# Feed-forward blocks of a Conformer layer: VectorE's work placed block by block, step d one block later, two buffers for normalised keys, chunk 1 transposed on TensorE

## The chip, the cores and the metric

The kernel runs on one core of a Trainium2 chip. Time is device microseconds of one launch, from its start to the last store. The core has five engines that each run their own instructions strictly in program order: TensorE (PE, matmuls), VectorE (DVE), ScalarE (ACT, activations), GpSimd (POOL) and SyncE (SP, which here issues nearly all DMAs). They meet through semaphores; in this kernel a small layer of code (class `Sync`) derives each wait from the buffers that an operation reads and writes.

## The reference

One Conformer layer over B = 2 sequences of T = 4000 tokens, D = 512 features, F = 2048 hidden, bf16 inputs. `ln` is a layer norm without weights.

```python
h  = silu(ln(x) @ w_ff1_a) @ w_ff1_b;   x1 = x + 0.5 * h        # first feed-forward
h  = ln(x1);  q, k, v = h @ w_q, h @ w_k, h @ w_v
p  = softmax(q @ k.T * D ** -0.5);      x2 = x1 + (p @ v) @ w_o # attention over all 4000 tokens
h  = ln(x2) @ w_pw1;  h = h[:, :D] * sigmoid(h[:, D:])
dc = depthwise_conv3(h);  dc = (dc - mean) / sqrt(var + 1e-5)   # mean, var over all tokens
x3 = x2 + silu(dc) @ w_pw2
h  = silu(ln(x3) @ w_ff2_a) @ w_ff2_b;  x4 = x3 + 0.5 * h       # second feed-forward
return ln(x4)
```

## The kernel before

**Tiles, chunks, stages.** A tile is 127 tokens; a chunk is four tiles, 508 tokens; there are 16 chunks (the last has three tiles). The stages follow each other: first feed-forward (ff1) over chunks 0 to 15, attention over 16 query groups with the convolution beside it, a short stretch that finishes the convolution, second feed-forward (ff2) over chunks 0 to 15 with swish and pointwise product (pw2) of later chunks beside it.

**Blocks and ticks.** A feed-forward chunk (`ff_chunk`, L1075) is a loop over 16 blocks, f = 0 to 15. In a block the function emits TensorE's products with their evictions, then calls the stage's `hook(f)`, then `tick()` (L589). `after(n, fn)` (L580) puts `fn` on a list that the n-th tick from now empties; an `after(5)` called in the hook of block 1 is emitted at the end of block 5. Nothing is reordered later: what is emitted first stands first in its engine's queue. An instruction that waits holds up all that is emitted behind it on the same engine.

**Fast chunks.** Chunks 2 to 14 of ff1 and 1 to 14 of ff2 compute both matrix products by a Winograd scheme with seven products in place of eight. The first product of a chunk is done in four quads (`ff_quad`, L994), one per group of four blocks. With g = PSUM bank 6, h = bank q % 2, e = bank 3 and x = bank 2, a quad has four steps:

- step a: product 1 into g (PE output named y); ScalarE copies g to h (`s<-y`); product 5 into e; ScalarE copies e to m5 (`sums<-s`).
- step b: product 2 into g; SiLU of g (`keys<-y`); product 6 into h; a tick later VectorE adds x = h + m5 (`s<-s,sums`, L1026).
- step c: product 7 into h, product 3 into x, SiLU of x (`keys<-s`); a tick later VectorE adds m5 = h + m5 (`sums<-s,sums`, L1026) and ScalarE takes SiLU of m5 (`keys<-sums`).
- step d: product 4 into h, SiLU of h (`keys<-s`).

Bank 6 is used by every quad: product 1 of a quad waits until ScalarE has taken the SiLU of g of the quad before. Product 4 waits for the sum m5, products 7 and 3 for the sum x. Steps a and b are emitted in blocks 0 and 2 of a group, c and d in blocks 1 and 3 of the next one (`ff_chunk`, `ff_pending`). Each product is four matmuls of 254 columns.

The second product of a chunk runs during the next chunk, as 14 units of eight matmuls of 256 columns (`ff_units`, L907) on banks 4 and 5, popped in the blocks listed in `ticks`; after a product's second unit VectorE adds the result into x or a temporary (L945), which also frees the bank. The units read sums that VectorE makes of the hidden activations (`ff_sums`, L893), of weights (`ff_weights`, L881) and, for the first product, of the transposed input (`ln_sums`, L982).

**Layer norms.** `ln_job` (L748) spreads the norm of one chunk over ticks: statistics of four tiles on VectorE (L721), four aggregates on VectorE (L726) with a power on GpSimd (L728), a shift on VectorE (L733), then one norm per tile on ScalarE (L658) or VectorE (L740). Kind "in" makes the next chunk's input: each normalised tile is transposed by a DMA (L666) into `lnT`. Kind "key" normalises the finished x1 for attention into `h2` and stores it to memory (`store_keys`, L833). `out_job` (L1660) is the like for the kernel's output. `h2` is one buffer of four tiles in region C at oQ1; a q-projection buffer of attention lies at the same place.

In ff1 and ff2 the input job is started in the hook of block 1 with `at` = 1: statistics at the ends of blocks 1 and 2 (two tiles each), the aggregate at 3, the shift at 4, two norms at 5 and two at 6. The key or output job is started by `done`, at the end of the chunk's second product (the tick of block 15 of the chunk after), with `at` = 8: statistics at the ends of blocks 7 and 8, norms at 11 and 12. Other hook work: loads of x, the fetch of stored x (`get_x`, ff2, block 0), key projections (ff1, second half), the swishes of ff2 (blocks 0 to 3, ScalarE) and pw2 with its residual (L856, VectorE; blocks 6, 8, 10, 12).

Of the kernel before, what the change touches and what calls it, by code (L numbers as in the profile page):

```python
# [8 lines left out]
ALU = mybir.AluOpType  # L9
# [249 lines left out]
class Conformer:  # L259
# [16 lines left out]

    def __init__(self, nc, ins, out):
        self.nc = nc
        self.i = ins
        self.x_flat = ins["x"].rearrange("b t d -> (b t) d")  # L280
        self.out_flat = out.rearrange("b t d -> (b t) d")
        self.S = Sync(nc)
        self.rings = {}
        self.memory()


    def memory(self):
# [134 lines left out]
        self.h2 = [C.view(oQ1 + j * 1024, D) for j in range(TPC)]  # L422
        self.b_h2 = [C.buf("h2", oQ1 + j * 1024, 1024) for j in range(TPC)]
        self.h2c = C.view(oQ1, TPC * D).rearrange("p (t d) -> p t d", t=TPC)
# [323 lines left out]
    def ln_job(self, c, at, kind, eng="DVE", gap=1, slot=None):  # L748

        sl = self.nxt("ln", self.LN_SLOTS)  # L750
        n = token_tiles(c) if slot is None else TPC

        def tile(ti):
            if kind == "key":
                self.ln_norm(c, sl, ti, self.h2[ti][0:TILE, :], self.b_h2[ti], eng)
                if ti == n - 1:
                    self.store_keys(c)
                return
# [4 lines left out]
            self.transpose(feat, tok, [b_tok], [b_feat])  # L763

        for ti in range(n):
            self.after(at + ti // 2 * gap, lambda ti=ti: self.ln_stats(c, sl, ti))
        self.after(at + 2 * gap, lambda: self.ln_aggr(sl, n))
        if eng == "ACT":
            self.after(at + 3 * gap, lambda: self.ln_shift(sl, n))
        for ti in range(n):  # L770
            self.after(at + (4 + ti // 2) * gap, lambda ti=ti: tile(ti))
# [61 lines left out]
    def store_keys(self, c):  # L833
# [7 lines left out]
        put(self.pieces(c, flat, self.h2c), self.b_h2, [self.b_keysd[c]] + (self.b_keyst if c == TCB - 1 else []))  # L841
        if c == TCB - 1:
            for b in range(B):
                e = b * HALF + TAIL
                put([(self.tailsd[b, r:r + REST, :], self.h2[TPC - 1][e - REST:e, :]) for r in range(0, 128, REST)],
                    [self.b_h2[TPC - 1]], [self.b_tailsd[b]])
# [34 lines left out]
    def ff_weights(self, st, step):  # L881
# [5 lines left out]
        todo = (((t1, b12, b11, ALU.subtract, [], n1), (t3, b22, b12, ALU.subtract, [], n3)),  # L887
                ((t2, t3, b11, ALU.add, n3, n2), (t4, b21, t2, ALU.subtract, n2, n4)))[step]
        for out, x, y, op, rd, wr in todo:
            self.S.op("DVE", lambda e, out=out, x=x, y=y, op=op: e.tensor_tensor(out=out, in0=x, in1=y, op=op),  # L890
                      reads=rd + self.b_Wb, writes=wr)

    def ff_sums(self, c, st, g, step):  # L893
# [7 lines left out]
        todo = (((s1, a21, a22, ALU.add, b1 + b2, n1), (s2, s1, a11, ALU.subtract, n1 + b1, n2)),  # L901
                ((s4, a12, s2, ALU.subtract, b2 + n2, n4), (s3, a11, a21, ALU.subtract, b1, n3)))[step]
        for out, x, y, op, rd, wr in todo:
# [3 lines left out]
    def ff_units(self, c, st, done, fast):  # L907
# [51 lines left out]
        else:  # L959
            ticks = [0, 1, 2] + list(range(4, 11)) + [12, 13, 14]  # L960
            if not self.fast[c + 1]:
                ticks = [0] + list(range(3, 15))
# [95 lines left out]
    def ff_around(self, c, f, st):  # L1058

        if f in ((3, 5) if self.fast[c - 1] else (1, 2)) and c:  # L1060
            self.ff_sums(c - 1, st, 1, int(f in (2, 5)))
# [3 lines left out]
    def ff_pending(self, f):  # L1065

        if self.quad and f in (1, 3):
            self.quad[2 + f // 2]()
            if f == 3:
                self.quad = None  # L1070
# [4 lines left out]
    def ff_chunk(self, c, st, hook, done):  # L1075

        fast = self.fast[c]
        at = (12, 13) if fast else (9, 10)
        for f in range(FC):
            self.ff_ring(c, f)  # L1080
            q, r = divmod(f, 4)
            if not fast:
                self.ff_block(c, f, st)
            elif r == 0:
                new = self.ff_quad(c, q, st)
                new[0]()
            elif r == 2:
                new[1]()
            elif self.quad:
                self.quad[2 + r // 2]()  # L1090
            if fast and r == 3:
                self.quad = new
            self.ff_around(c, f, st)
            if f in at:
                self.ff_sums(c, st, 0, f - at[0])
            if c == 0 and f in (12, 13):
                self.ff_weights(st, f - 12)
            if f in (10, 11) and self.fast[c + 1]:
                self.ln_sums(c + 1, f - 10)
# [7 lines left out]
    def ff_plain(self, c, st, hook, done):  # L1107
# [4 lines left out]
        for f in range(FC):  # L1112
            self.ff_ring(c, f)
            p = st.late[f % len(st.late)]
            self.ff_first(c, f, *p)
            self.ff_pending(f)
# [15 lines left out]
    def ff_last(self, c, st):  # L1132
# [4 lines left out]
        for f in range(FC):  # L1137
            self.ff_ring(c, f)
            self.ff_first(c, f, *blocks[f])
            self.ff_pending(f)  # L1140
# [519 lines left out]
    def out_job(self, c, at):  # L1660
        sl = self.nxt("ln", self.LN_SLOTS)
        for ti in range(TPC):
            self.after(at + ti // 2, lambda ti=ti: self.ln_stats(c, sl, ti))
        self.after(at + 2, lambda: self.ln_aggr(sl, TPC))
        self.after(at + 3, lambda: self.ln_shift(sl, TPC))

        def tile(ti):
            g = c * TPC + ti
            self.ln_norm(c, sl, ti, self.XT[g], self.bx[g], "ACT")
            if ti == TPC - 1:  # L1670
                self.store_out(c, 0, TPC)

        for ti in range(TPC):
            self.after(at + 4 + ti // 2, lambda ti=ti: tile(ti))
# [395 lines left out]
```

## Time and profile before

| | us |
|---|---|
| runs of the kernel (three) | 1985.48, 1989.34, 1991.63 |
| median | 1989.34 |
| profiled execution | 1989.63 |
| its span (first to last instruction) | 1985.7 |
| TensorE busy in the span | 1951.8 |
| ff1, 60 to 450 us: TensorE, VectorE, ScalarE busy | 381.50, 299.43, 269.81 |
| attention, 500 to 1420 us: the same | 920.00, 611.93, 313.89 |
| ff2, 1560 to 1920 us: the same | 357.33, 296.92, 267.69 |

The profile is of one execution, about 4 us shorter in its span than that execution's device time. A group of the profile is named by the line of a helper: every matmul is L608 and every activation L658, so groups are told apart by the tiles that they write and read (`y<-work,wff`, `keys<-sums`). "Busy" of TensorE counts modelled ends; a hole of a few hundred ns between starts of matmuls may not show in it.

### The profile page before, as it was taken

What the parts mean: (1) busy time and instruction counts of PE and PEld (TensorE: products, weight loads), DVE (VectorE), ACT (ScalarE), POOL (GpSimd) and SP (SyncE); (2) the same over time, 40 slices, a digit from 0 to 9 for tenths busy, and PEclk for the clock granted to TensorE, in tenths of its full rate; (3) what the DMA queues carried; (4) which work ended last, traced back from release to release, by engine and by line L of the source; (5) the groups of instructions that cost most, each with busy time, mean ns of one, the idle gap of its engine ahead of it and who ended that gap; (6) DMA issues with size and microseconds to landing.
All of it is one profiled execution on the core that took longest, in us unless ns stands there. A gap on an engine that the chain in (4) does not pass through costs nothing.

```text
span 1985.7 us, 31983 instructions
## 1 busy us (share of the span) xinstructions
PE 1951.8 (98%) x12610; PEld 1252.9 (63%) x12610; DVE 1412.4 (71%) x2738; ACT 1004.2 (51%) x1728; POOL 109.1 (5%) x235
## 2 busy tenths in 40 slices
PE   8999999999999999999999999999999999999998
PEld 5889988963444444444444444444455788888887
DVE  6688888844566676667766766676687788888885
ACT  4677777743333333333333333333337677777775
POOL 1000000000000000000000000000002000000000
PEclk9999999999999999999999999999999999999999
DMA  9233344344211221223532212211135222322211
GB/s 191 64 85 86 78 98 93 73 128 125 83 37 28 52 59 25 49 53 85 128 67 54 56 27 49 51 49 36 45 105 148 61 65 64 84 55 55 50 41 42
DMA packets 272620, 140.12 MB, mean 71 GB/s; under 512 B 204744, under 2 KB 263819, under 8 KB 272463
## 3 DMA queue, kind: packets, MB, share of 16 engines
q1 hardware_dynamic: 271785, 137.67, 28.6%
q8 instruction: 101, 1.65, 0.3%
q14 instruction: 56, 0.46, 0.1%
q10 hardware_dynamic: 678, 0.34, 0.1%
HBM read 53.26 MB, written 39.20 MB: 47 GB/s over the span
## 4 chain that ended last, share of the span: by engine, by line
PE 83%; DVE 10%; DMA 2%; issue 1%; SPq 1%; POOL 1%; ACT 1%; DVEq 0%; POOLq 0%; ACTq 0%
PE s L608 43%; PE y L608 40%; DVE work L721 3%; DVE keys L904 2%; DVE sums L1026 1%; DMA work<-work 1%; DVE s L1026 1%; POOL work L728 1%; SPq L662 1%; DVE sums L991 0%; DMA keysd<-work 0%; DMA wff<-in_w_ff_b_dram 0%; DVE work L945 0%; DVE keys L945 0%; ACT work L658 0%
## 5 line engine op out<-in xcount | busy, mean ns | idle before, releaser
L608 PE MATMUL y<-work,keys 128*127 128x256 bf16 (+2 forms) x3904 | 746.6, 324 | 2.5 <-DVE work L945 1.5
L658 ACT ACTIVATE work<-s 128x508 bf16<-128x508 f32 (+2 forms) x543 | 317.8, 587 | 641.2 <-PE s L608 629.4
L608 PEld LDWEIGHTS y<-work,keys 128*128 128x128 bf16 (+1 forms) x3904 | 407.3, 117 | 243.6 <-DVE work L945 5.9
L1299 DVE TENSOR_TENSOR work<-work 128x508 f32<-128x508 f32 (+1 forms) x480 | 324.2, 675 | 263.0 <-ACT work L658 260.0
L608 PE MATMUL s<-work,keys 128*128 128x508 bf16 (+2 forms) x2240 | 506.9, 357 | 4.4 <-ACT work L658 4.4
L608 PEld LDWEIGHTS s<-work,keys 128*128 128x128 bf16 (+1 forms) x2240 | 195.6, 97 | 234.3 <-ACT work L658 11.2
L658 ACT ACTIVATE keys<-s 128x508 bf16<-128x508 f32 (+1 forms) x281 | 163.3, 584 | 156.5 <-PE s L608 155.0
L608 PE MATMUL y<-wff,keys 128*127 128x256 bf16 (+3 forms) x1592 | 210.8, 282 | 0.2 <-DVE xt L945 0.2
L608 PE MATMUL s<-sums 128*128 128x254 bf16 x1296 | 194.5, 273 | 4.1 <-DVE s L1026 3.0
L721 DVE BATCH_NORM_STATS2 work<-xt 127x6 f32<-127x512 bf16 x311 | 195.4, 680 | 3.5 <-DMA xt<-in_x_dram 3.4
L608 PE MATMUL s<-work,wff 128*128 128x508 bf16 (+4 forms) x884 | 189.2, 354 | 8.4 <-DMA work<-work 5.9
L608 PEld LDWEIGHTS y<-wff,keys 128*127 128x127 bf16 (+1 forms) x1592 | 175.5, 136 | 19.4 <-issue 7.1
L904 DVE TENSOR_TENSOR keys<-keys 128x1016 bf16<-128x1016 bf16 x240 | 158.8, 682 | 7.1 <-ACT keys L658 4.3
L658 ACT ACTIVATE work<-xt,work 127x512 bf16<-127x512 bf16 x179 | 135.6, 805 | 21.7 <-DVE work L733 14.5
L608 PE MATMUL s<-work 128*127 128x512 bf16 (+4 forms) x569 | 144.2, 379 | 1.2 <-DVE work L1713 1.2
L608 PEld LDWEIGHTS s<-sums 128*128 128x128 bf16 x1296 | 126.5, 98 | 23.2 <-DVE s L1026 3.5
L608 PEld LDWEIGHTS s<-work,wff 128*128 128x128 bf16 x884 | 81.1, 98 | 90.6 <-issue 12.3
L728 POOL TENSOR_TENSOR work<-work 127x4 f32<-127x4 f32 (+1 forms) x76 | 77.6, 1022 | 1083.0 <-DVE work L726 1083.0
L608 PE MATMUL y<-work,wff 128*128 128x254 bf16 (+1 forms) x892 | 135.4, 274 | 1.0 <-ACT keys L658 1.0
L1026 DVE TENSOR_TENSOR sums<-s,sums 128x508 f32<-128x508 f32 x108 | 72.7, 674 | 44.7 <-PE s L608 44.7
L608 PEld LDWEIGHTS s<-work 128*127 128x127 bf16 (+2 forms) x569 | 66.3, 119 | 59.0 <-issue 3.6
L608 PEld LDWEIGHTS y<-work,wff 128*128 128x128 bf16 x892 | 86.9, 98 | 10.8 <-ACT keys L658 1.6
(129 smaller groups left out, 1575.5 us busy)
## 6 DMA issues: line engine op xcount, KB each, us to landing
xd<-xt SPq DMA_DIRECT2D x28, 448.0 KB, 2.9
xt<-xd SPq DMA_DIRECT2D x28, 448.0 KB, 3.7
keys<-keysd SPq DMA_DIRECT2D x62, 128.0 KB, 2.5
keysd<-work SPq DMA_DIRECT2D x14, 448.0 KB, 3.0
out_dram<-xt SPq DMA_DIRECT2D x14, 448.0 KB, 3.2
dcvd<-wff SPq DMA_DIRECT2D x48, 127.0 KB, 1.9
keys<-dcvd SPq DMA_DIRECT2D x12, 508.0 KB, 5.8
xt<-in_x_dram SPq DMA_DIRECT2D x13, 448.0 KB, 5.2
```

Source lines behind the costliest of these rows:

```text
L608: self.S.op("PE", lambda e: e.matmul(out, lhsT, rhs, start=start, stop=stop, **kw), reads=reads, writes=[bank], inc=stop if inc is None el ...
L658: return self.S.op("ACT", lambda e: e.activation(out, in_, func, **kw), reads=reads, writes=writes)
L662: return self.S.dma(eng, k, lambda e: e.dma_start(dst, src), reads=reads, writes=writes)
L721: self.S.op("DVE", lambda e: e.bn_stats(self.st[sl][:, ti, 0:6], x), reads=[b_x], writes=[self.b_st[sl][ti]])
L728: S.op("POOL", lambda e: e.tensor_tensor(out=self.rs[sl][:, 0:n], in0=self.mv[sl][:, 0:n, 1], in1=self.neghalf[0:TILE, 0:n], op=ALU.pow), ...
L904: self.S.op("DVE", lambda e, out=out, x=x, y=y, op=op: e.tensor_tensor(out=out, in0=x, in1=y, op=op), reads=rd, writes=wr)
L1026: S.op("DVE", lambda e: e.tensor_tensor(out=out, in0=h[:, W], in1=m5, op=ALU.add), reads=[b_h, b_m5], writes=[b_out])
L1299: S.op("DVE", lambda e, p=p: e.tensor_tensor(out=acc, in0=acc, in1=self.P[p][:, 0:W], op=ALU.add), reads=[self.b_P[p], self.b_acc[s]], wri ...
```

## The change

- `ln_job` takes a plan of ten tick numbers (four statistics, aggregate, shift, four norms) in place of `at` and `gap`, and takes over `out_job`. Two plans are used in fast chunks: IN for the input job, now started in the hook of block 0, and OUT for the key and output jobs. With IN, statistics come at the ends of blocks 0, 1, 4 and 4, the aggregate at 6, the shift and two norms at 8, two norms at 9. With OUT, counted from the tick of block 15, two statistics come at block 8, two at 12, the aggregate at 14, the shift in block 0 of the chunk after and the four norms in its blocks 1 to 4, one each.
- Step d goes from block 3 of the next group to block 0 of the one after it, ahead of that group's step a (`ff_chain`).
- `ff_sums` and `ff_weights` are issued singly or in pairs at other blocks, `ln_sums` at blocks 14 and 15 (before 10 and 11).
- `h2` becomes two buffers, by the parity of the chunk: one at oQ1 in region C, one in region E behind m5.
- Chunk 1 of ff1: its norms stay on VectorE, but the four tiles are transposed by 16 TensorE transposes, with two copies each on ScalarE and VectorE, four ticks after the norms.
- `get_x` of ff2 moves to block 8. The first key projections (`key_rest`) come two steps later. The output norms of ff2's chunk 14 are done by VectorE.

The core of the diff:

```diff
+    IN = (1, 2, 5, 5, 7, 9, 9, 9, 10, 10)
+    OUT = (9, 9, 13, 13, 15, 17, 18, 19, 20, 21)
+
     def __init__(self, nc, ins, out):
...
-        self.h2 = [C.view(oQ1 + j * 1024, D) for j in range(TPC)]
-        self.b_h2 = [C.buf("h2", oQ1 + j * 1024, 1024) for j in range(TPC)]
-        self.h2c = C.view(oQ1, TPC * D).rearrange("p (t d) -> p t d", t=TPC)
+        homes = ((C, oQ1), (E, 28672))
+        self.h2 = [[R.view(o + j * 1024, D) for j in range(TPC)] for R, o in homes]
+        self.b_h2 = [[R.buf("h2", o + j * 1024, 1024) for j in range(TPC)] for R, o in homes]
+        self.h2c = [R.view(o, TPC * D).rearrange("p (t d) -> p t d", t=TPC) for R, o in homes]
...
-    def ln_job(self, c, at, kind, eng="DVE", gap=1, slot=None):
+    def ln_job(self, c, kind, eng="DVE", plan=(1, 1, 2, 2, 3, 4, 5, 5, 6, 6), slot=None, pe=None):
...
         n = token_tiles(c) if slot is None else TPC
+        stats, aggr, shift, norm = plan[0:4], plan[4], plan[5], plan[6:10]
...
             if kind == "key":
-                self.ln_norm(c, sl, ti, self.h2[ti][0:TILE, :], self.b_h2[ti], eng)
+                self.ln_norm(c, sl, ti, self.h2[c % 2][ti][0:TILE, :], self.b_h2[c % 2][ti], eng)
                 if ti == n - 1:
                     self.store_keys(c)
+                return
+            if kind == "out":
+                g = c * TPC + ti
+                self.ln_norm(c, sl, ti, self.XT[g], self.bx[g], eng)
+                if ti == n - 1:
+                    self.store_out(c, 0, TPC)
                 return
...
             self.ln_norm(c, sl, ti, tok[0:TILE, :], b_tok, eng)
-            self.transpose(feat, tok, [b_tok], [b_feat])
+            if pe:
+                self.after(4, lambda: self.transpose_pe(ti, s, pe[ti], self.bank(4 + ti)))
+            else:
+                self.transpose(feat, tok, [b_tok], [b_feat])
         for ti in range(n):
-            self.after(at + ti // 2 * gap, lambda ti=ti: self.ln_stats(c, sl, ti))
-        self.after(at + 2 * gap, lambda: self.ln_aggr(sl, n))
+            self.after(stats[ti], lambda ti=ti: self.ln_stats(c, sl, ti))
+        self.after(aggr, lambda: self.ln_aggr(sl, n))
         if eng == "ACT":
-            self.after(at + 3 * gap, lambda: self.ln_shift(sl, n))
+            self.after(shift, lambda: self.ln_shift(sl, n))
         for ti in range(n):
-            self.after(at + (4 + ti // 2) * gap, lambda ti=ti: tile(ti))
+            self.after(norm[ti], lambda ti=ti: tile(ti))
...
-        put(self.pieces(c, flat, self.h2c), self.b_h2, [self.b_keysd[c]] + (self.b_keyst if c == TCB - 1 else []))
+        h2, b_h2 = self.h2[c % 2], self.b_h2[c % 2]
+        put(self.pieces(c, flat, self.h2c[c % 2]), b_h2, [self.b_keysd[c]] + (self.b_keyst if c == TCB - 1 else []))
         if c == TCB - 1:
...
                 e = b * HALF + TAIL
-                put([(self.tailsd[b, r:r + REST, :], self.h2[TPC - 1][e - REST:e, :]) for r in range(0, 128, REST)],
-                    [self.b_h2[TPC - 1]], [self.b_tailsd[b]])
+                put([(self.tailsd[b, r:r + REST, :], h2[TPC - 1][e - REST:e, :]) for r in range(0, 128, REST)],
+                    [b_h2[TPC - 1]], [self.b_tailsd[b]])
...
         n1, n2, n3, n4 = [[b] for b in st.b_w]
-        todo = (((t1, b12, b11, ALU.subtract, [], n1), (t3, b22, b12, ALU.subtract, [], n3)),
-                ((t2, t3, b11, ALU.add, n3, n2), (t4, b21, t2, ALU.subtract, n2, n4)))[step]
-        for out, x, y, op, rd, wr in todo:
-            self.S.op("DVE", lambda e, out=out, x=x, y=y, op=op: e.tensor_tensor(out=out, in0=x, in1=y, op=op),
-                      reads=rd + self.b_Wb, writes=wr)
-
-    def ff_sums(self, c, st, g, step):
+        out, x, y, op, rd, wr = ((t1, b12, b11, ALU.subtract, [], n1), (t3, b22, b12, ALU.subtract, [], n3),
+                                 (t2, t3, b11, ALU.add, n3, n2), (t4, b21, t2, ALU.subtract, n2, n4))[step]
+        self.S.op("DVE", lambda e: e.tensor_tensor(out=out, in0=x, in1=y, op=op), reads=rd + self.b_Wb, writes=wr)
+
+    def ff_sums(self, c, st, g, steps):
...
         n1, n2, n3, n4 = [[b[g]] for b in st.b_s]
-        todo = (((s1, a21, a22, ALU.add, b1 + b2, n1), (s2, s1, a11, ALU.subtract, n1 + b1, n2)),
-                ((s4, a12, s2, ALU.subtract, b2 + n2, n4), (s3, a11, a21, ALU.subtract, b1, n3)))[step]
-        for out, x, y, op, rd, wr in todo:
+        todo = ((s1, a21, a22, ALU.add, b1 + b2, n1), (s2, s1, a11, ALU.subtract, n1 + b1, n2),
+                (s4, a12, s2, ALU.subtract, b2 + n2, n4), (s3, a11, a21, ALU.subtract, b1, n3))
+        for out, x, y, op, rd, wr in [todo[n] for n in steps]:
             self.S.op("DVE", lambda e, out=out, x=x, y=y, op=op: e.tensor_tensor(out=out, in0=x, in1=y, op=op),
...
         else:
-            ticks = [0, 1, 2] + list(range(4, 11)) + [12, 13, 14]
-            if not self.fast[c + 1]:
-                ticks = [0] + list(range(3, 15))
+            ticks = [0] + list(range(3, 15))
         return [lambda n=n, g=g: unit(n, g) for n, g in order], ticks
...
-        if f in ((3, 5) if self.fast[c - 1] else (1, 2)) and c:
-            self.ff_sums(c - 1, st, 1, int(f in (2, 5)))
+        if c and f in (3, 7):
+            self.ff_sums(c - 1, st, 1, (0, 1) if f == 3 else (2, 3))
+        if c and f == 0 and self.fast[c - 1]:
+            self.ff_sums(c - 1, st, 0, (2,))
         if st.units and f in st.ticks:
...
-    def ff_pending(self, f):
-
-        if self.quad and f in (1, 3):
-            self.quad[2 + f // 2]()
-            if f == 3:
-                self.quad = None
+    def ff_chain(self, f):
+
+        if f % 4 == 0 and self.fourth:
+            self.fourth()
+            self.fourth = None
+        if f % 4 == 1 and self.third:
+            self.third[2]()
+            self.fourth, self.third = self.third[3], None
...
         fast = self.fast[c]
-        at = (12, 13) if fast else (9, 10)
+        own = {11: (0, 1), 12: (3,)} if fast else {9: (0, 1), 10: (2, 3)}
         for f in range(FC):
...
             q, r = divmod(f, 4)
+            self.ff_chain(f)
             if not fast:
...
             elif r == 0:
-                new = self.ff_quad(c, q, st)
-                new[0]()
+                quad = self.ff_quad(c, q, st)
+                quad[0]()
             elif r == 2:
-                new[1]()
-            elif self.quad:
-                self.quad[2 + r // 2]()
-            if fast and r == 3:
-                self.quad = new
+                quad[1]()
+            elif r == 3:
+                self.third = quad
             self.ff_around(c, f, st)
-            if f in at:
-                self.ff_sums(c, st, 0, f - at[0])
-            if c == 0 and f in (12, 13):
+            if f in own:
+                self.ff_sums(c, st, 0, own[f])
+            if c == 0 and f > 11:
                 self.ff_weights(st, f - 12)
-            if f in (10, 11) and self.fast[c + 1]:
-                self.ln_sums(c + 1, f - 10)
+            if f > 13 and self.fast[c + 1]:
+                self.ln_sums(c + 1, f - 14)
             if f == FC - 1:
...
             self.ff_ring(c, f)
+            self.ff_chain(f)
             p = st.late[f % len(st.late)]
             self.ff_first(c, f, *p)
-            self.ff_pending(f)
             self.ff_around(c, f, st)
...
             self.ff_ring(c, f)
+            self.ff_chain(f)
             self.ff_first(c, f, *blocks[f])
-            self.ff_pending(f)
             self.ff_around(c, f, st)
-    def out_job(self, c, at):
...
         self.out_evs = []
-        self.ring, self.quad = list(range(4)), None
+        self.ring, self.third, self.fourth = list(range(4)), None, None
         self.place(0, self.slot(0))
...
             for k in range(self.PRELOAD, 28):
-                yield 6, lambda k=k: self.key_queries(0, k)
+                yield 8, lambda k=k: self.key_queries(0, k)
             for k in range(15):
...
                     self.load_x(c + 2)
-                if f == 1 and c + 1 < NCK:
-                    self.ln_job(c + 1, 1, "in", "ACT" if c else "DVE")
+                if f == 0 and c + 1 < NCK:
+                    if c:
+                        self.ln_job(c + 1, "in", "ACT", self.IN)
+                    else:
+                        self.ln_job(c + 1, "in", "DVE", (1, 1, 2, 2, 3, 3, 9, 9, 9, 9), pe=("ACT", "DVE", "ACT", "DVE"))
                 if c == 1 and f in (4, 5, 6, 7):
...
                 self.put_x(c)
-                self.ln_job(c, 8 if c < NCK - 2 else 2 if c < NCK - 1 else 5, "key", "ACT")
+                self.ln_job(c, "key", "ACT", self.OUT if c < NCK - 2 else
+                            (2, 2, 3, 3, 4, 6, 6, 6, 7, 7) if c < NCK - 1 else (5, 5, 6, 6, 7, 9, 9, 9, 10, 10))
...
         def projected(g):
-            self.ln_job(g, 1, "in", slot=0)
+            self.ln_job(g, "in", slot=0)
             self.after(3, lambda: self.put_x(g))
...
                 n = c + AHEAD
-                if f == 0 and n + 1 < NCK:
+                if f == 8 and n + 1 < NCK:
                     self.get_x(n + 1, self.slot(n + 1))
...
                         self.pw2_residual(n, [ti], bank)
-                if f == 1 and c + 1 < NCK:
-                    self.ln_job(c + 1, 1, "in", "ACT")
-
-            self.ff_chunk(c, second, hook, lambda: self.out_job(c, 8 if c < NCK - 2 else 1))
+                if f == 0 and c + 1 < NCK:
+                    self.ln_job(c + 1, "in", "ACT", self.IN)
+
+            def done():
+                if c < NCK - 2:
+                    self.ln_job(c, "out", "ACT", self.OUT)
+                else:
+                    self.ln_job(c, "out")
+
+            self.ff_chunk(c, second, hook, done)
```

More of the change, by code (lines that the diff above doesn't have):

```diff
@@ L1657, in pw2_residual @@
             self.residual(ps[0:TILE, :], b_ps, t * TPC + ti, 1.0)
-    def out_job(self, c, at):
[L1661 to L1674, printed above, removed]
     def fold_weights(self):
```

## The prediction, made before the changed kernel was run

> **What bounds the kernel now.** I read the busy shares, then a table by stage, then TensorE's waits, then the order of single instructions in one feed-forward chunk.
>
> ```profile
> PE 1951.8 (98%) x12610; PEld 1252.9 (63%) x12610; DVE 1412.4 (71%) x2738; ACT 1004.2 (51%) x1728; POOL 109.1 (5%) x235
> ```
>
> TensorE is the bound; VectorE and ScalarE matter only where they make it wait. The table by stage (stretch, its length, then busy us of each engine, the granted clock, DMA share, GB/s):
>
> ```profile
> 0.00:60.00 60.00, 52.27 (x330) 32.24 (x331) 36.94 (x83) 27.50 (x49) 5.57 (x17) 0.94 0.76 158
> 60.00:450.00 390.00, 381.50 (x3246) 334.72 (x3245) 299.43 (x630) 269.81 (x461) 29.41 (x29) 1.00 0.38 91
> 450.00:500.00 50.00, 45.57 (x219) 19.95 (x218) 19.90 (x35) 16.47 (x29) 1.19 (x1) 0.97 0.43 119
> 500.00:1420.00 920.00, 920.00 (x4579) 426.79 (x4577) 611.93 (x1070) 313.89 (x548) 28.59 (x114) 1.00 0.23 55
> ...
> 1560.00:1920.00 360.00, 357.33 (x3020) 315.59 (x3019) 296.92 (x609) 267.69 (x454) 24.23 (x24) 1.00 0.24 60
> ```
>
> The reader is to see that attention has no hole and that the change works in the other stages. Their ScalarE is loaded to 69% (269.81/390) and 74% (267.69/360), VectorE to 77% and 82%: far from full, so order decides. "Busy" hides small holes, since matmul ends are modelled. Starts of successive matmuls are 109 ns apart at 254 or 256 columns and 216 ns at 508; a fast chunk of the first stage has 224 narrow ones, 24.42 us, yet chunks 4 to 8 follow each other at 25.29 us, later ones at up to 27.2. By the same count, starts beyond these rates lose 16.9 us in 60 to 450 and 9.2 us in 1560 to 1935 (a chunk there: 27.9 us of matmuls, measured 28.43).
>
> TensorE's waits by releaser (total, times, longest) name what can go:
>
> ```profile
> PE s L608 <- DVE sums L1026: 6.0, 19, 1.0
> PE s L608 <- DMA work<-work: 5.9, 1, 5.9
> PE s L608 <- ACT work L658: 5.0, 3, 2.6
> PE s L608 <- DVE s L1026: 3.0, 2, 2.4
> PE s L608 <- DVE xt L856: 1.6, 1, 1.6
> PE y L608 <- ACT keys L658: 1.0, 2, 0.5
> ```
>
> The last is product 1 of a group, waiting for the SiLU that frees its bank (step b of the group before). It is small here; I forecast that it grows. The timeline of one chunk shows ScalarE's order around that SiLU:
>
> ```profile
> 251.52 0.17 DVE L733 SCALAR_TENSOR_TENSOR work<-work 127x4 f32<-127x4 f32 x1 [1.19 <-POOL work L728]
> 251.72 1.52 ACT L658 ACTIVATE work<-xt,work 127x512 bf16<-127x512 bf16 x2 [0.38 <-DVE work L733]
> 253.51 0.63 ACT L658 ACTIVATE keys<-sums 128x508 bf16<-128x508 f32 x1 [0.27 <-DVE sums L1026]
> 254.04 0.58 ACT L658 ACTIVATE keys<-y 128x508 bf16<-128x508 f32 x1
> 254.51 0.80 ACT L658 ACTIVATE work<-xt,work 127x512 bf16<-127x512 bf16 x1
> 255.05 0.38 PE L608 MATMUL y<-work,wff 128*128 128x254 bf16 x2
> ```
>
> One pair of norms stands ahead of that SiLU (keys<-y, 254.04), the second pair behind it, and product 1 (255.05) is in time.
>
> **The change, part by part.**
>
> *Start-up.* Chunk 1's transposes leave the DMA for TensorE: the 5.88 us wait at 29.63 goes, and the half clock after it (508-wide matmuls at 427 ns from 30.0 to 34.3, about 2.65 us). Added: 16 transposes of 127 columns, like the head's at L623, about 0.9 us with their gaps. Two of the four copies sit on VectorE behind the first weight sum, which waits for the weights until 23.63 and lasts 1.2; copies of 0.68 then end near 25.7, so a wait of about 1.4 us stays. Moving matmuls from 29.63 to 25.9 with 2.65 of half clock gone: −6.4 (−7 to −5).
>
> *First stage, what goes.* Step d moves one block later, so the sum m5 (L1026) is no longer awaited; statistics, sums and norms get blocks with fewer rivals, so the holes that VectorE makes, 16.9 us, go (at least 12, if only the listed waits and the growth after chunk 9 go).
>
> *First stage, what comes.* IN puts the four norms at the ends of blocks 8 (two) and 9 (two); the code puts step c's SiLU of x between the pairs, and SiLU m5 and SiLU g behind both. ScalarE works in order, so product 1 of block 12 waits for norm pair 1.41 (back to back; 1.52 with its start), SiLU 0.49, pair 1.41, SiLUs 0.51 and 0.58, hand-over 0.05: 4.45 us from the first norm. That norm follows the shift by 0.20; VectorE reaches the shift after block 6's add, two sums of block 7 and two statistics of the store job (0.60 each): 0.42 us after block 8's end. TensorE reaches product 1 after blocks 9 and 10 (16 matmuls each), an empty block 11 and step d's four: 36 × 0.109 = 3.92. Wait: 0.42 + 4.45 − 3.92 = 0.95 per chunk. Twelve chunks, and 0.25 in the one before the three-tile chunk: +11.7 (bounds: 0, if VectorE is a microsecond earlier, to +23, if it is one later). Stage: −16.9 + 11.7 = −5.2.
>
> *Start of attention.* Two homes for normalised keys take away the waits at 458.40 and 468.04 (1.99 and 2.77 with hand-over, 6.7 with the half clock after the second). One store (0.92 to 1.25 on SP's queue) now precedes the query transposes that were issued at 455.59; issued about 456.6 and 4.35 us to landing, they are there at 460.95, TensorE at 458.13: a wait of 2.8, perhaps with its own half clock. Taken −3 (−5 to −1).
>
> *Opening of the last stage.* Waits behind late sums (L856, L1026: 1.81 and 2.56) go, 0.45 returns for the first sums: −3.9 (−5 to −2).
>
> *Last stage, steady.* Its 9.2 us go. In their place the same chain on ScalarE, started later: the pointwise product beside block 8 ends, hand-over 0.20, residual 0.61 (L856), two statistics 1.20, shift and hand-over 0.20: the first norm 2.21 after it. 2.21 + 4.45 = 6.66 against 44 narrow matmuls, 4.80: a wait of 1.9 in chunks 2 to 13, 0.66 in chunk 1, 0.25 in chunk 14: 23.7. ScalarE also has four swishes (0.71) and the output norms, now one a block, in blocks 0 to 4: 0.2 at block 4 and 0.3 at block 6 in eleven chunks, 5.5. The aggregate ahead of the add that unit (4,0) needs: 0.32 in thirteen, 4.2. Together +33.4 against −9.2: +24.2 (bounds: 0, if the chain finds slack, to +40).
>
> *The rest.* Sums of weights, one a block, lie beside matmuls that do not read them yet; fetching x at block 8 is still a whole chunk ahead; the second-last chunk's norms on VectorE cost 0.1 at the end. If the weights' cover went, one sum (1.23) would be the price.
>
> Sum: −6.4 − 5.2 − 3.0 − 3.9 + 24.2 + 0.1 = +5.8 on the profiled execution's 1989.63 (span 1985.7), which stands 0.3 above the runs' median: 1995.4, rounded 1995.5.
>
> *The clock.* The trace halved it after 5.88 us idle and after 2.60 us at 468.04, which came 10 us after 1.82; not after 1.82 at 458.40 nor 2.40 at 1557.36. The forecast waits of 1.9 lie with those that did not. [...]
>
> **The rivals.**
> 1. *ScalarE's queue clears in time* (faster): no new wait at block 12, only removals. For it: ScalarE is idle a quarter of these stages. Against it: its order is fixed. 1989.63 − 6.4 − 16.9 − 3 − 3.9 − 9.2 = 1950. Decides if the first norm starts 1.9 us before my count.
> 2. *The first norm is one microsecond earlier* than counted, as VectorE runs ahead: the first stage's 11.7 goes and twelve of the 23.7: 1972. For it: shorter VectorE work (0.39 for an aggregate, norms away from it). Against: in the last stage the residual cannot precede its product.
> 3. *Waits that halve the clock* each chunk: about 1.8 us more (as after 468.04) in twelve chunks: 2017. Against: 1.99 and 2.56 alone did not.
> 4. *The change does not do what it says*: VectorE's holes move but stay, and only start-up and attention gain, lost again on ScalarE: 1990.
>
> **How the numbers follow.** Forecast 0.60, rivals 0.10, 0.18, 0.06 and 0.06. The likeliest's own range is 1983 to 2006. Leaving out rival 1, rival 3 and small tails gives 1970 to 2008. A measurement of this kernel tells no less than 0.3%, 6 us, from no change (bounds 1983.4 and 1995.3): the forecast's mass lies 0.04 under, 0.20 within, 0.36 above, since waits that I did not count can only add. Faster 0.04 + 0.10 + 0.18 = 0.32; same 0.20 + 0.06 = 0.26; slower 0.36 + 0.06 = 0.42.
>
> **What would show it.** Right: TensorE's waits led by product 1 (y) released by ScalarE's SiLU, some 35 us in all, 0.95 a chunk in the first stage and 1.9 in the last; chunk periods of 25.4 and 30.6; no wait on L1026; matmuls of chunk 1 from 25.9 at full clock. Wrong: periods of 24.4 and 28 with no SiLU wait (rival 1), 427 ns matmuls inside chunks (rival 3), or the query transposes landing before 458.

## The result and the profile after

The changed kernel takes 1995.2 us (median of 8 runs, 1993.94 to 1998.71) against 1988.15 us before (8 runs, 1985.48 to 1991.63): ratio 1.0037, 95% interval 1.0025 to 1.0049. It is slower by a third of a per cent. The profiled execution took 1994.55 us with a span of 1990.5, 4.8 more than before's.

TensorE's waits in the profile after (in total, times, longest) are led by another engine than before:

```profile
PE y L612 <- ACT keys L662: 27.8, 25, 1.7
PE y L612 <- ACT s L662: 3.1, 10, 1.1
PE s L612 <- DMA work<-keysd: 3.1, 1, 3.1
PE y L612 <- DVE work L958: 1.8, 12, 0.2
```

L612 is the matmul, L662 the activation, L958 the units' add (L608, L658 and L945 before). The waits for L1026, 9.0 us in 21 places before, are gone; the wait for the SiLU of g (`keys`), 1.0 us before, is now 27.8. The second and the fourth line are smaller waits of the last stage, at blocks 6 and 8. The table by stage (stretch, length, busy us of each engine, clock, DMA share, GB/s) shows that the stages went opposite ways:

```profile
0.00:60.00 60.00, 58.08 (x399) 37.38 (x403) 39.46 (x89) 33.70 (x62) 5.23 (x17) 1.00 0.68 167
...
1560.00:1920.00 360.00, 334.47 (x2805) 292.34 (x2804) 278.34 (x570) 250.05 (x424) 23.22 (x23) 1.00 0.22 57
```

Start-up rose from 52.27 us of TensorE work in 60 to 58.08; the last stage fell from 357.33 in 360 to 334.47. Counted by starts of matmuls beyond 109 and 216 ns (transposes by TensorE count as lost), the losses of each stage are as follows. For the kernel before, the prediction's own counts are 16.9 us in 60 to 450 and 9.2 us in 1560 to 1935.

| stage | lost before, us | lost after, us | difference | forecast |
|---|---|---|---|---|
| start-up, to 60 us | 16.9 | 9.6 | −7.2 | −6.4 |
| first stage, from 60 us | 17.7 | 10.3 | −7.4 | −5.2 |
| start of attention | 6.8 | 5.1 | −1.7 | −3.0 |
| 1420 to 1560 us | 8.2 | 5.0 | −3.2 | −3.9 |
| last stage, from 1560 us | 10.4 | 35.0 | +24.7 | +24.2 |

One place that recurs in the chunks of the last stage, product 1 of block 12, carries most of the loss: 21.2 of 35.0 us. The timeline there in one chunk, of VectorE, ScalarE and TensorE (start, length, engine, line, operation, output and input; in brackets the idle time of the engine before it and what ended it):

```profile
1634.37 0.69 DVE L871 SCALAR_TENSOR_TENSOR xt<-y,xt 127x512 bf16<-127x512 f32 x1 [0.85 <-PE y L612]
1634.97 1.28 DVE L725 BATCH_NORM_STATS2 work<-xt 127x6 f32<-127x512 bf16 x2
1636.17 0.15 DVE L737 SCALAR_TENSOR_TENSOR work<-work 127x4 f32<-127x4 f32 x1
1636.35 1.52 ACT L662 ACTIVATE work<-xt,work 127x512 bf16<-127x512 bf16 x2 [3.20 <-DVE work L737]
1637.78 0.57 ACT L662 ACTIVATE keys<-s 128x508 bf16<-128x508 f32 x1
1638.25 1.51 ACT L662 ACTIVATE work<-xt,work 127x512 bf16<-127x512 bf16 x2
1639.66 0.61 ACT L662 ACTIVATE keys<-sums 128x508 bf16<-128x508 f32 x1
1640.18 0.57 ACT L662 ACTIVATE keys<-y 128x508 bf16<-128x508 f32 x1
1640.81 0.61 PE L612 MATMUL y<-work,wff 128*128 128x254 bf16 x4 [1.68 <-ACT keys L662]
```

Read it upwards. Product 1 of block 12 (1640.81) waits 1.68 us for the SiLU of g at 1640.18, whose input has long been there; it stands behind two norm pairs and two other SiLUs. The first of these norms waits for the shift at 1636.17, and the shift stands on VectorE behind a residual, which waits for the pointwise product beside block 8, and two statistics. Before it ScalarE was idle for 3.20 us: the engine that makes TensorE wait was itself waiting. From the first norm to product 1 it is 4.46 us.

### The profile page after: what moved, and what is told of

It reads as the page before. It is cut to its first block, busy times and chain, and to the rows that moved or that the text cites. A ratio compares the mean times of both kernels' runs of the same rounds, so it can differ in the third digit from the quotient of the medians.

```text
span 1990.5 us, 31987 instructions
## 1 busy us (share of the span) xinstructions
PE 1945.2 (98%) x12623; PEld 1253.3 (63%) x12626; DVE 1419.2 (71%) x2743; ACT 1000.4 (50%) x1726; POOL 108.7 (5%) x235
## 4 chain that ended last, share of the span: by engine, by line
PE 91%; DVE 4%; ACT 3%; SPq 1%; issue 1%; DMA 0%; POOL 0%; POOLq 0%; DVEq 0%; ACTq 0%
PE y L612 45%; PE s L612 45%; DVE xt L871 1%; ACT work L662 1%; DVE s L1037 1%; ACT keys L662 1%; DVE work L958 1%; DVE keys L917 1%; ACT xt L662 1%; DVE xt L958 1%; SPq L666 0%; ACT s L662 0%; DVE work L725 0%; SPq L670 0%; DMA work<-keysd 0%
## 5 line engine op out<-in xcount | busy, mean ns | idle before, releaser
L612 PE MATMUL y<-work,keys 128*127 128x256 bf16 (+2 forms) x3904 | 740.6, 324 | 1.9 <-DVE work L958 1.8
L662 ACT ACTIVATE work<-s 128x508 bf16<-128x508 f32 (+2 forms) x543 | 318.0, 587 | 638.3 <-PE s L612 634.1
L612 PEld LDWEIGHTS y<-work,keys 128*128 128x128 bf16 (+1 forms) x3904 | 407.5, 117 | 237.7 <-DVE work L958 5.9
L612 PE MATMUL s<-work,keys 128*128 128x508 bf16 (+2 forms) x2240 | 506.6, 357 | 0.0
L612 PEld LDWEIGHTS s<-work,keys 128*128 128x128 bf16 (+1 forms) x2240 | 195.9, 97 | 229.3 <-ACT work L662 5.8
L662 ACT ACTIVATE keys<-s 128x508 bf16<-128x508 f32 (+1 forms) x281 | 163.3, 585 | 185.0 <-PE s L612 163.0
L612 PE MATMUL y<-wff,keys 128*127 128x256 bf16 (+3 forms) x1592 | 209.2, 281 | 0.1
L612 PE MATMUL s<-sums 128*128 128x254 bf16 x1296 | 194.4, 273 | 0.0
L612 PE MATMUL s<-work,wff 128*128 128x508 bf16 (+4 forms) x884 | 187.7, 352 | 0.6 <-ACT work L662 0.2
L612 PEld LDWEIGHTS y<-wff,keys 128*127 128x127 bf16 (+1 forms) x1592 | 175.9, 136 | 17.5 <-issue 6.6
L612 PE MATMUL y<-work,wff 128*128 128x254 bf16 (+1 forms) x892 | 135.8, 275 | 31.4 <-ACT keys L662 27.8
L612 PE MATMUL s<-work 128*127 128x512 bf16 (+4 forms) x569 | 144.5, 379 | 5.1 <-DMA work<-keysd 3.1
L612 PEld LDWEIGHTS s<-sums 128*128 128x128 bf16 x1296 | 126.8, 98 | 18.1
L662 ACT ACTIVATE work<-xt,work 127x512 bf16<-127x512 bf16 x148 | 112.9, 804 | 44.9 <-DVE work L737 43.1
L612 PEld LDWEIGHTS s<-work,wff 128*128 128x128 bf16 x884 | 80.9, 98 | 81.2 <-issue 4.0
L612 PEld LDWEIGHTS y<-work,wff 128*128 128x128 bf16 x892 | 83.1, 98 | 53.6 <-ACT keys L662 38.2
L612 PEld LDWEIGHTS s<-work 128*127 128x127 bf16 (+2 forms) x569 | 66.3, 119 | 63.5 <-issue 3.8
L1037 DVE TENSOR_TENSOR s<-s,sums 128x508 f32<-128x508 f32 x108 | 74.1, 686 | 31.6 <-ACT keys L662 18.8
```

Of the source, the lines that this page charges most:

```text
L612: self.S.op("PE", lambda e: e.matmul(out, lhsT, rhs, start=start, stop=stop, **kw), reads=reads, writes=[bank], inc=stop if inc is None el ...
L662: return self.S.op("ACT", lambda e: e.activation(out, in_, func, **kw), reads=reads, writes=writes)
L1037: S.op("DVE", lambda e: e.tensor_tensor(out=out, in0=h[:, W], in1=m5, op=ALU.add), reads=[b_h, b_m5], writes=[b_out])
```

## The experiments

Ratios are to the kernel before, timed on the same chip beside the runs of its group. Its median there was 1989.09 us beside e1 to e4, 1991.22 beside e5 to e8, 1990.05 beside e9 to e11 and 1989.15 beside e12, against 1988.15 beside the changed kernel: a difference of 3 us between medians of different groups shows nothing by itself.

| run | median, us | ratio, 95% interval |
|---|---|---|
| e1_shift_early | 1972.44 | 0.9921 [0.9905, 0.9938] |
| e2_norms_single | 1973.79 | 0.9926 [0.9908, 0.9944] |
| e3_before_late_norms | 2003.93 | 1.0075 [1.0058, 1.0092] |
| e4_d_block3 | 1995.0 | 1.0027 [1.0015, 1.004] |
| e5_both | 1968.72 | 0.9894 [0.9874, 0.9914] |
| e6_one_h2 | 2004.18 | 1.0069 [1.0053, 1.0086] |
| e7_dma_chunk1 | 2002.14 | 1.0061 [1.0044, 1.0078] |
| e8_fetch_early | 1996.24 | 1.0028 [1.0014, 1.0041] |
| e9_group1_early | 1995.65 | 1.0029 [1.0018, 1.004] |
| e10_three_ahead | 1968.51 | 0.9893 [0.9878, 0.9908] |
| e11_out_late | 1958.37 | 0.9843 [0.9829, 0.9856] |
| e12_keys13_early | 1954.63 | 0.9823 [0.981, 0.9836] |

### Where the wait comes from: e1 to e4

```diff
-    IN = (1, 2, 5, 5, 7, 9, 9, 9, 10, 10)
+    IN = (1, 2, 5, 5, 7, 8, 9, 9, 10, 10)
```

> The changed kernel with the shift of the input job one block earlier (end of block 7 instead of block 8), nothing else. Theory (the first norm comes late because VectorE reaches the shift behind a residual and two statistics, and four norms then stand ahead of the SiLU that product 1 of block 12 waits for): the norms start as soon as ScalarE has done block 8's copies, 0.7 us earlier in the first stage and about 3.4 us earlier in the second; the waits of 0.85 shrink to about 0.15 and those of 1.85 vanish: 11 x 0.7 + 11 x 1.85 + 0.9 = 29 us less, about 1966 us. Rival (ScalarE has too much to do between blocks 8 and 12, so the wait only moves): waits stay or turn up elsewhere, 1985 us or more.

One number moved a shift of 0.15 us by one block, and 22.8 us went (1995.2 to 1972.44; 29 were expected). The same place of the last stage, in the timeline of this run:

```profile
1629.25 0.15 DVE L737 SCALAR_TENSOR_TENSOR work<-work 127x4 f32<-127x4 f32 x1
1629.44 1.52 ACT L662 ACTIVATE work<-xt,work 127x512 bf16<-127x512 bf16 x2 [0.47 <-DVE work L737]
1630.18 0.69 DVE L871 SCALAR_TENSOR_TENSOR xt<-y,xt 127x512 bf16<-127x512 f32 x1 [0.78 <-PE y L612]
...
1633.48 0.57 ACT L662 ACTIVATE keys<-y 128x508 bf16<-128x508 f32 x1
1634.78 0.60 PE L612 MATMUL y<-work,wff 128*128 128x254 bf16 x4
```

The shift is now ahead of the residual, ScalarE's idle time shrinks from 3.20 to 0.47 us, and the SiLU is done before product 1 needs it: the waits of 1.85 at block 12 are gone. In the first stage they fell from 0.85 to 0.63 only, where 0.15 was expected. The reason stands in that stage's timeline, of the same run:

```profile
119.60 0.16 DVE L737 SCALAR_TENSOR_TENSOR work<-work 127x4 f32<-127x4 f32 x1
120.76 1.51 ACT L662 ACTIVATE work<-xt,work 127x512 bf16<-127x512 bf16 x2
```

The norm follows the shift by 1.16 us without a bracket: ScalarE was busy with block 8's copies, so the four norms and three SiLUs are what is left of the wait.

```diff
-    IN = (1, 2, 5, 5, 7, 9, 9, 9, 10, 10)
+    IN = (1, 2, 5, 5, 7, 9, 9, 10, 11, 12)
```

> The changed kernel with the four input norms one a block (ends of blocks 8, 9, 10, 11) instead of two and two at 8 and 9; the shift stays. Theory: only two norms (0.80 each) stand ahead of the SiLU instead of two pairs (1.41 each), 1.2 us less: the 0.85 of the first stage vanish, the 1.85 of the last become about 0.63; 9.3 + 12 x 1.2 = 24 us less, about 1971 us. Rival (what decides is when the shift comes, not how many norms follow): waits of the last stage stay above 1.5, about 1985 us.

21.4 us less, 24 expected. The waits of the last stage fell from 1.85 to 0.44; those of the first vanished in most chunks (about 0.45 to 0.49 stayed in a few, where the later norms delayed the first sums). So the wait of the last stage needs both a late first norm and a long queue, and removing either takes most of it away. In the first stage the queue counts for more: the early shift took 0.22 of 0.85, the spread norms nearly all.

The reverse was tried on the kernel before (the shift at the end of block 8, norms at 8 and 9, first sums at 14 and 15; the jobs of both stages are called with `late=3`):

```diff
-            self.after(at + 3 * gap, lambda: self.ln_shift(sl, n))
+            self.after(at + 3 * gap + late + (late > 0), lambda: self.ln_shift(sl, n))
...
-            self.after(at + (4 + ti // 2) * gap, lambda ti=ti: tile(ti))
+            self.after(at + (4 + ti // 2) * gap + late, lambda ti=ti: tile(ti))
```

> The kernel before with only its input norms moved as the change has them (shift and two norms at the end of block 8, two at block 9; first sums of the transposed input at blocks 14 and 15 so that they don't wait for it). Theory: the SiLU waits at block 12 come with the norms alone, about 0.9 a chunk in the first stage and 1.8 in the last, on top of VectorE's old holes, less a few us that the late sums give back: about 2012 us (2004 to 2018). Rival (they come from VectorE's new layout or the later step d): no such waits, about 1988 us.

Its waits of TensorE, first line:

```profile
PE y L608 <- ACT keys L658: 28.7, 27, 1.7
```

28.7 us against 27.8 in the changed kernel, 0.84 a chunk in the first stage and 1.85 in the last: the moved norms, with the first sums behind them, bring the wait without any other part of the change. The total was 8 us below the expectation. What I had not reckoned with is that the same move also removes VectorE's holes: beside its waits of product 1 the first stage lost about 5 us instead of 17.7 and the last about 6 instead of 10.4. So most of the gain that the prediction spread over step d, statistics, sums and norms already comes with the later norms and first sums. Whether the move removes the holes or the new waits give VectorE time to catch up, e3 alone doesn't show; in e12 below, where most of these waits are gone too, the first stage lost 4.9 us and the last 4.4, so with all of the new layout the holes stay away.

In e4 only step d of the changed kernel was moved back:

```diff
-        if f % 4 == 0 and self.fourth:
+        if f % 4 == 3 and self.fourth:
```

> The changed kernel with step d back at block 3 of the next group. If the later step d is what took away the waits for the sum m5: these come back, about 0.37 us in some two dozen blocks, +9 us, about 2004 us. Theory (VectorE reaches m5 in time now, since statistics and sums lie elsewhere): no waits on m5, 1995 to 1997 us.

No wait on m5 came back, and the time did not change (1995.0 against 1995.2). So the later step d is worth nothing here; in the last stage it even costs a little (with step d back, the wait at block 6 fell from 0.39 to 0.24 us in most chunks). Without the SiLU waits, as in e12, it was not tried.

### The parts that stand alone: e6 to e9

> The changed kernel with chunk 1's norms transposed by DMA again, normalised at the ends of blocks 4 and 5 (one block earlier than before). Theory: the DMA wait ahead of chunk 1 comes back with 4.5 to 6 us and the half clock behind it with about 2.6, less the 0.9 us of transposes on TensorE: +6 us, about 2001 us. Rival (start-up gained from the sums of weights spread over four blocks): 1995 to 1997 us.

The edit calls `ln_job(c + 1, "in", "DVE")` for chunk 1, without TensorE's transposes. The timeline of TensorE:

```profile
27.40 1.05 PE L612 MATMUL s<-work,wff 128*128 128x508 bf16 x4 [4.02 <-DMA work<-work]
28.26 1.90 PE L612 MATMUL y<-wff,keys 128*127 128x256 bf16 x8
29.95 3.61 PE L612 MATMUL s<-work,wff 128*128 128x508 bf16 x12
```

The median rose by 7 us (6 expected): a wait of 4.0 us came back, and eight matmuls of 256 columns took 1.90 us where 1.04 is usual, the half clock. Not all of it is the transposes' worth: in the trace, start-up lost 5.7 us more in waits and half clock for 0.9 us of transposes less, a net 4.8, and the other 2.5 us arose at the start of attention (a wait of 1.0 us, the rest a longer half clock), which nothing ties to this edit. So the transposes on TensorE are worth about 5 us to the changed kernel.

```diff
-        homes = ((C, oQ1), (E, 28672))
+        homes = ((C, oQ1), (C, oQ1))
```

> The changed kernel with one home for normalised keys, as before. If the second home is worth what its waits cost before (1.99 + 2.77 and the half clock, 6.7 us in all): about 2002 us. Theory (the start of attention still loses 3.2 us and half clock to the late query transposes, so most of the gain was given back): the old waits come in place of that one, +1 to +3 us, about 1997 us.

Neither expectation's mechanism was right, though the larger one's time was (2004.18 against 2002). The old waits of 1.99 and 2.77 did not come back; one of 9.31 did, and a second of 1.69 at 462.68. TensorE and ScalarE in the timeline:

```profile
443.98 1.87 PE L612 MATMUL s<-work,keys 128*128 128x508 bf16 x4 [9.31 <-ACT work L662]
441.93 1.52 ACT L662 ACTIVATE work<-xt,work 127x512 bf16<-127x512 bf16 x2 [13.03 <-DMA keysd<-work]
```

OUT pushes chunk 13's key norms into attention's first key tiles, so with one home chunk 14's norms wait for chunk 13's store. The second home is worth some 8 us to the new plan, which made the need (in the trace the start of attention lost 13 us instead of 5; the medians differ by 9); against the kernel before, this stretch gained 1.7 us.

The late transpose at the start of attention cost more than it took to read. The profile after (SP, then TensorE):

```profile
441.62 2.64 SPq L670 DMA_TRANSPOSE work<-keysd  x1
446.35 1.88 PE L612 MATMUL s<-work 128*128 128x508 bf16 x4 [3.09 <-DMA work<-keysd]
448.02 1.66 PE L612 MATMUL s<-work,keys 128*128 128x508 bf16 x4
```

> The changed kernel with the transposed fetch of the first queries issued at block 3 of the last chunk of the first stage instead of block 12, ahead of SP's store of x and the loads of keys behind it. Theory (TensorE's 3.1 us wait at the start of attention is SP's queue alone): wait and half clock go, 3.2 + 1.6 = 4.8 us, about 1990 us. Rival (the next thing that attention needs, keys or the norms' stores, is as late): 1 or 2 us less at most, 1993.5 us or more.

Nothing changed (1996.24), since I moved the wrong fetch: this transpose is that of query group 1, issued in the loop of group 0, and the fetch of group 0 was early enough all along. The next run moved the right one:

```diff
-                if g + 1 < NCK and g != 1 and 7 <= kt < 7 + TPC:
-                    self.fetch_queries((g + 1) // TCB, (g + 1) % TCB, kt - 7)
+                if g + 1 < NCK and g != 1 and kt == (7 if g else 1):
+                    self.fetch_queries((g + 1) // TCB, (g + 1) % TCB, 0)
```

> The changed kernel with the transposed fetch for query group 1 issued at key tile 1 of group 0 instead of key tile 7, ahead of a store of keys and several loads on SP. The run with group 0's fetch moved showed that its wait was not this one: the transpose issued at 441.62 is that of group 1. Theory: TensorE's wait of 3.1 us and the half clock behind it go, about 4.8 us, about 1990.5 us. Rival (that transpose itself waits for a buffer or a store): 1994 us or more.

The wait for the transpose went, and its half clock (four matmuls of 508 columns take 1.02 us there, against 1.88 in the profile after); another took its place, in the waits of this run:

```profile
PE s L612 <- ACT work L662: 2.9, 3, 2.1
```

The stretch lost 2.4 us less in the profile, which the times don't show (1995.65, interval 1.0018 to 1.004). What waits now is the exponential of a key tile behind a norm of chunk 15's keys; e12 takes that up.

### Towards a faster kernel: e5, e10 to e12

> The changed kernel with both edits: shift at the end of block 7 and the four input norms one a block, ends of blocks 8 to 11. Theory (in the first stage the first norm now starts when ScalarE has done block 8's copies, and two norms stand ahead of the SiLU instead of four): the 0.63 a chunk that the early shift alone left go, 10 x 0.63 + 0.85 = 7 us less than with the early shift alone, about 1965 us. Rival (the last two norms push the SiLU behind step d and the copies of block 12, or the transposes come too late for the sums at block 14): new waits of 0.3 or more a chunk, 1972 us or more.

IN = (1, 2, 5, 5, 7, 8, 9, 10, 11, 12) gave 1968.72, 3.7 us below e1 where 7 were expected: what the rival names came true in part, though not its time. VectorE's waits in the first stage, of this run:

```profile
DVE sums L1002 <- DMA work<-work: 4.9, 5, 2.1
```

The changed kernel has no such line there, and e1 one of 0.3: the last norm is now so late that its transpose has not landed when the first sums of block 14 want it, and TensorE's waits of 0.42 and 0.49 follow in some of the later chunks.

> Early shift (end of block 7), input norms two at block 8, one at 9, one at 10 (three ahead of the SiLU, and the last one block earlier than in the run with one a block), and group 1's fetch early. Theory: ScalarE's chain to product 1 of block 12 is 0.6 us shorter than with the early shift alone, so its waits of 0.63 go (7 us), with at most 2 us back where the last transpose delays the first sums; 4.8 us from the fetch: about 1962 us (1960 to 1965). Rival: the late transposes cost as much as in the run with one norm a block, 1964 to 1968 us.

IN = (1, 2, 5, 5, 7, 8, 9, 9, 10, 11) and the fetch of e9: 1968.51, the rival again. The waits of 0.63 of the first stage went, but its sums still waited for transposes, 6.7 us in four places, and at the start of attention 3.6 us were lost to the norm that e9 had uncovered.

The edit of e11, against e10:

```diff
-    IN = (1, 2, 5, 5, 7, 8, 9, 9, 10, 11)
+    IN = (1, 2, 5, 5, 6, 8, 9, 9, 10, 11)
...
-                    self.ln_job(c, "out", "ACT", self.OUT)
+                    self.ln_job(c, "out", "ACT", (9, 9, 13, 13, 15, 17, 20, 21, 22, 23))
```

> As the run with three norms ahead, and two more edits: the aggregate of the input job one block earlier (block 5) and the output norms of the last stage at the ends of blocks 4 to 7, behind the swishes, instead of 1 to 4 beside them. Theory: the waits of 0.32 at block 8 (VectorE's add behind the aggregate, 13 chunks) and of 0.19 and 0.39 at blocks 4 and 6 (ScalarE's queue) go: 4 + 6.5 us, about 1952 us. Rival (the norms only move the queue): product 1 of block 8 waits instead, 0.5 or more a chunk, 1958 us or more.

1958.37, 10 us less than e10, as the theory had it (it expected 1952 from a starting point of 1962). The time alone lies in the rival's range, but the rival's waits at block 8 did not come. The waits of 0.32 at block 8 and of 0.19 and 0.39 at blocks 4 and 6 went but for a few; the last stage lost 3.3 us in 1560 to 1920, where e10 lost 13.5 and the changed kernel 34.4.

The edit of e12, against e11:

```diff
-                self.ln_job(c, "key", "ACT", self.OUT if c < NCK - 2 else
+                self.ln_job(c, "key", "ACT", self.OUT if c < NCK - 3 else
+                            (8, 8, 9, 9, 10, 11, 12, 12, 13, 13) if c < NCK - 2 else
```

> As the run with the output norms behind the swishes, and chunk 13's keys normalised within chunk 15 (statistics at its blocks 7 and 8, norms at 11 and 12, as before the change) instead of in attention's first key tiles. In that run TensorE still waited 2.25 us at the start of attention, with half clock behind it: ScalarE's norm of chunk 15's keys waits 7.1 us for the store of chunk 13's, which shares its home and stands on SP behind eight transposes and loads. Theory: that store is done early, wait and half clock go, 2.25 + 1.8 = 4 us, about 1954 us. Rival (the norms of chunk 15 wait for their own statistics or for the store of x next): 1957 us or more.

ScalarE's norms of chunk 15's keys, first in e11, then in e12:

```profile
437.46 1.52 ACT L662 ACTIVATE sums<-xt,work 127x512 bf16<-127x512 bf16 x2 [7.13 <-DMA keysd<-sums]
```

```profile
432.11 1.52 ACT L662 ACTIVATE sums<-xt,work 127x512 bf16<-127x512 bf16 x2 [2.13 <-DVE work L737]
```

The wait for chunk 13's store is gone; TensorE has no hole left at the start of attention. 1954.63 us: 3.7 us below e11 (the intervals of the two ratios touch, but the profiled span fell from 1952.8 to 1948.5 us as well), 1.8% below the kernel before (ratio 0.9823, 0.981 to 0.9836) and about 2% below the changed one. What TensorE still waits for in e12:

```profile
PE y L612 <- ACT keys L662: 1.3, 4, 0.3
PE s L612 <- DVE work L1710: 1.2, 1, 1.2
PE s L612 <- DMA work<-in_dw_dram: 1.0, 1, 1.0
```

## Why the prediction was right

It said 1995.5 and slower as likeliest; 1995.2 was measured. The mechanism that it named, ScalarE's queue ahead of the SiLU of g, is what made TensorE wait. That the total is so close is luck in part: the stages miss by up to 2.2 us each, in both directions (−5.2 forecast in the first stage, −7.4 measured; −3.0 and −1.7 at the start of attention). Step by step:

- **ScalarE's chain** of 4.45 us from the first norm to product 1 measured 4.46; the first norm 2.21 us after the pointwise product measured 2.18 (1636.35 less 1634.17, when the fourth matmul of 0.216 us after 1633.31 was through). e1, e2 and e3 show that it is this chain and its late start, not a neighbour of it.
- **First stage.** The wait was 0.85 in eleven chunks, 9.3 us, where 0.95 in twelve was counted, 11.7; chunk 2 had none. VectorE's holes went but for about 1 us. What was attributed wrongly is why: e4 shows that the later step d did nothing, while in e3 the later norms and first sums alone came with most of it.
- **Last stage.** Block 12: 11 × 1.85 + 0.9 = 21.2 against 23.7, since chunk 2 waited 0.9 and not 1.9 and chunks 1 and 14, forecast at 0.66 and 0.25, not at all. Blocks 4 and 6: about 8 us against 5.5 (0.19 + 0.39 in most chunks, but 2.0 once, in the chunk whose swishes come in twos). Block 8: 0.32 in thirteen, as counted. Two errors of 2.5 us cancel; the sum is not better known than that. The period of a chunk, named as a sign, was 25.31 us in the first stage (25.4 forecast) and 30.74 in the last (30.6).
- **Start-up.** The half clock (granted clock 1.00 in the first 60 us, 0.94 before) and the DMA wait went. Of the wait of 1.4 us for VectorE's copies 0.2 was left in the profile after, up to 1.8 in the experiments' profiles; what makes it differ was not tried.
- **Start of attention.** A wait of 2.8 us was forecast, 3.1 came, with a half clock that was left open (from 445.89 to 449.30, 1.7 us lost). Which fetch it was I had not checked, as e8 showed.
- **The rivals.** "The first norm one microsecond earlier", 1972, agrees with the 1972.4 of e1 only by chance: it took 11.7 us from the first stage and 12 from the last, while e1 took about 2 from the first and 21 from the last. "The queue clears in time", 1950, is near what e12 reached, 1954.6, but e12 has other edits too. None of the waits of 1.85 us was followed by half clock: the granted clock of the profile after is 1.00 in 1560 to 1920 us.

## What to carry to other kernels

An engine that is half idle on average (ScalarE here, busy 50% of the span after) can still be the bound: on in-order engines ask, for each moved instruction, what then stands ahead of the next one that the bound engine waits for, and follow the queue back to its first late member. That member may be tiny (a shift of 0.15 us) and sit on a third engine; issuing it before the instructions that wait there cost nothing in e1. A plan that is later for everything also moves the last chunks' work into the stage that follows, where buffers and the DMA queue are shared.

## What was not expected of the hardware

The same wait of 2.25 us at the same place of the program was followed by half clock on TensorE in one profile and not in another (the brackets show 2.09, counted from the modelled end of the matmul before; by starts of matmuls it is 2.25). In e11 (first fence) four matmuls of 508 columns after it take 1.90 us, in e9 (second fence) 1.02:

```profile
439.51 1.03 PE L612 MATMUL s<-work,keys 128*128 128x508 bf16 x4 [2.09 <-ACT work L662]
440.39 1.53 PE L612 MATMUL y<-work,keys 128*128 128x508 bf16 x4
441.71 1.90 PE L612 MATMUL s<-work 128*128 128x508 bf16 x4
```

```profile
444.47 1.03 PE L612 MATMUL s<-work,keys 128*128 128x508 bf16 x4 [2.09 <-ACT work L662]
445.34 1.02 PE L612 MATMUL y<-work,keys 128*128 128x508 bf16 x4
446.20 1.02 PE L612 MATMUL s<-work 128*128 128x508 bf16 x4
```

So the length of a wait alone did not decide here. By the brackets, the waits of 2.60 us at 468.04 (kernel before), 3.09 at 446.35 (changed kernel) and 9.31 at 443.98 (e6) were each followed by half clock, four matmuls of 508 columns taking 1.88, 1.88 and 1.87 us; the 2.40 us before 1557.36 that the prediction lists were not (granted clock 1.00 in 1530 to 1560 us), nor were the waits of 1.85 us at block 12 (1.68 in the bracket). What decides beside the length, these runs do not show.
